# Fused attention and feed-forward: a fourth chunk in seven products, attention paced by weight, weight sums at the ends of two chunks

## The chip, the core and the metric

The kernel runs on one core of one Trainium2 chip. The metric is device time in microseconds (us) of one execution. TensorE (PE) multiplies matrices; VectorE (DVE), ScalarE (ACT) and GpSimd (POOL) do element-wise work; SyncE (SP) issues most DMA transfers, and ScalarE some. Each engine has a queue of its own; they wait for each other by semaphores.

## The reference, cut to what matters

```python
k_p = k.reshape(B, H, Sp, pool, D).mean(axis=3)      # 8 x 8 heads, 576 rows pooled to 72, D = 64
v_p = v.reshape(B, H, Sp, pool, D).mean(axis=3)
scores = scale * np.matmul(q, k_p.transpose(0, 1, 3, 2))
attn = softmax(scores)                               # with 1e-09 added to the sum
x = np.matmul(attn, v_p) -> 4608 tokens x 512        # heads side by side
h = x @ w_in                                         # 512 x 2048
g = np.maximum(0.01 * h, h)
return g @ w_out                                     # 2048 x 512
```

All data is fp32.

## The kernel before

**Feed-forward.** The 4608 tokens go in nine chunks of 512 (`CH`), c = 0 to 8. The hidden features are 16 blocks `f` of 128. A product with fp32 accuracy is three matmuls on two parts of each number (`h` and `l`: high and low): high by high, high by low, low by high. For one `f`, `m1` (L1143 to L1145) makes `ph` in 12 matmuls of 512 columns; ACT applies the leaky step (L1148) and casts to `gh` (L1151), DVE forms `gl` (L1152); two blocks later `m2` adds the block to the four output sums `acc` through `add_up` (L1354 to L1356), 12 matmuls of 512 columns.

**Seven products.** For the last chunks `m1` is replaced: two blocks `f` form a pair (8 `PAIRS`), and a 2 by 2 product of half-size blocks is made with seven products in place of eight (`product`, L1261: six matmuls of 256 columns each, 42 a pair). It needs sums of the weights, made once by `prepare`: sums on DVE (L1183) in the spare buffer `x_tail`, a cast on ACT (`high`, L1186), a subtraction on DVE (`low`, L1190), and stores to `kept` in DRAM (L1217), four results of two parts a pair. They are read back into `seat`s and weight buffers by `stream` (L1253, issued by ACT). The first run with seven products is `REST + FAST - 1`.

**Runs.** The program is a list of runs n = 0 to 11, with REST = 4: n = 5 is chunk 2, n = 8 chunk 5 ("the sixth"), n = 11 chunk 8. So with FAST = 6 the runs n = 9, 10 and 11 use seven products.

**Attention** is made one or two chunks ahead, in steps that a run issues between its matmuls: `lk`, `ku`, `lv`, `vu` load and pool k and v (POOL L265, L272; `vremsum` are the pooled rows left over, `v_parts` L522 and L524 split them), `q` and `qa` load and turn q, `s` makes scores `pss` (L600) and `e` (L610), `sb` normalizes to `at` on POOL and stores it as `rows` (L661), which come back turned as `blocks` (L670; `at` and `blocks` share three buffers). `pu` transposes `blocks` to `pp` (DVE L681, a buffer of the pool `five`, tag "o", which output tiles use too) and splits it into `pT_hi` (ACT L703) and `pT_lo` (DVE L706, L710). `au` multiplies `pT` with v to `pa` (PE L725 to L728), named by piece and head pair (`pa_0_2`), and ACT (L744) and DVE (L745) split it into the next chunk's `xh`, `xl`.

**What sets the order.** PE runs in the order of the program text, and from the first run with seven products on POOL and SP too. The order on ACT, DVE and, before that, SP and POOL is fixed at the build. An engine then takes its instructions strictly in its order. A run with three plain products has 64 beats (a beat is a part of a matmul group, about 1.5 us), one with seven 96. `PLAN` says for a run how many pairs' sums `prepare` makes in it and between which beats. Attention's steps are spread over the run by their count: step i of m comes when the beat reaches i/m of the run.

```python
PLAN = {REST + 1: (2, 10, 36), REST + 2: (3, 3, 34), REST + 3: (1, 3, 20), REST + 4: (2, 3, 34)}
```

In all four runs the sums lie in parts of x buffers that `free` finds unused, and all of a pair's stores are issued behind its last `low`.

Of the kernel before, what the change touches and what calls it, by code (L numbers as in the profile page):

```python
# [10 lines left out]
F32 = mybir.dt.float32  # L11
F32R = mybir.dt.float32r
# [12 lines left out]
def tile_pooled_attention_ffn(  # L25
# [9 lines left out]
    nc = tc.nc  # L35

    P = 128
# [32 lines left out]
    VIA = 2  # L70
    SPLIT = 8
    HALF = CH // 2
    FAST = 6
    NEAR = (FAST + 1) % 2


# [1095 lines left out]
    def prepare(j, places):  # L1172

        f0, f1 = PAIRS[j]
        (a11, a12), (a21, a22) = (
            [[ws[0, f].bitcast(F32)[:, part, half] for part in range(2)]
             for half in (slice(0, HALF), slice(HALF, DM))] for f in (f0, f1)
        )
        u, w = (x_tail[:, 2 * i : 2 * i + 2, :].rearrange("p k x -> p (k x)") for i in range(2))
        ADD, SUB = ALU.add, ALU.subtract  # L1180

        def do(out, a, b, op):
            nc.vector.tensor_tensor(out, a, b, op=op)  # L1183

        def high(i, of):
            nc.scalar.copy(places[i][0], of)  # L1186

        def low(i, of):
            h, l = places[i]
            nc.vector.tensor_tensor(l, of, h.bitcast(F32), op=SUB)  # L1190

        do(u, a21[0], a21[1], ADD)
        do(w, u, a22[0], ADD)
        yield
        do(w, w, a22[1], ADD)
        high(1, w)
        do(u, a11[0], u, SUB)
        yield
        do(u, u, a11[1], ADD)
        high(0, u)  # L1200
        low(1, w)
        yield
        do(w, w, a11[0], SUB)
        low(0, u)
        yield
        do(w, w, a11[1], SUB)
        high(2, w)
        do(u, a12[0], w, SUB)
        yield
        do(u, u, a12[1], ADD)  # L1210
        high(3, u)
        low(2, w)
        yield
        low(3, u)
        for i, parts_of in enumerate(places):
            for k, part in enumerate(parts_of):
                nc.sync.dma_start(kept[j, :, i, k, :], part.bitcast(F32))  # L1217
        if j < OPEN:
            with tc.issue_after(sent[-1].ins):
                nc.sync.dma_start(kept[j, :, 4], ws[0, f1].bitcast(F32)[:, :, HALF:])  # L1220
        yield

    def free(n, i):

        if n < REST + FAST - 2:
            return [(h[:, HALF:], l[:, HALF:]) for h, l in zip(*x_parts(runs[n][0] + 1))]
        side, part = (runs[n][0] + 2) % 2, "hl"[i % 2]
        x = [one.tile([P, CH], F32R, tag=f"x{part}{side}_{kk}", name=f"place{i}_{kk}") for kk in range(NK)]
        return [(y[:, :HALF], y[:, HALF:]) for y in x]
# [230 lines left out]
    for b in range(2, B):  # L1460
        for j, piece in enumerate(PIECES[b]):
            c = 2 + (2 * TAIL + S * (b - 2) + piece[0][0]) // CH
            beside[REST + c - 2].append((b, j))
    units = []

    def line_of(n, pieces):
        start = REST + FAST - 1
# [38 lines left out]
    for b, n in loads_at.items():  # L1506
        early[max(n, REST) - 1].append(b)

    PLAN = {REST + 1: (2, 10, 36), REST + 2: (3, 3, 34), REST + 3: (1, 3, 20), REST + 4: (2, 3, 34)}
    STEPS_OF = 7  # L1510
    left = list(range(len(PAIRS)))

    def sums_in(n):
        for i in range(PLAN[n][0]):
            yield from prepare(left.pop(0), free(n, i))

    at = 0
    for n, (c, fs, ts) in enumerate(runs[: REST + FAST - 1]):
        us = list(units[n])
        final = n == REST + FAST - 2  # L1520
        steps_in = None
        if n >= REST:
            nxt = n - REST + 2
            if nxt in waiting:
                us.insert(0, lambda nxt=nxt: carry(nxt))
            mid = len(us) // 2
            for b in early[n]:
                us[mid:mid] = [att[b]["lk"], att[b]["lv"]]
            if n == REST:

                us.insert(3 * len(us) // 4, fetch)
        beats, done, beat = (2 + len(ts) // 2) * len(fs), 0, 0
        forming, formed = (sums_in(n), 0) if n in PLAN else (None, 0)
        many, begin, until = PLAN.get(n, (0, 0, 1))
        behind = 10 if final else 4
        for f in fs:
            if n == 0:
                convert_to(14 + 2.8 * f)
            elif n == 1:
                convert_to(36)  # L1540
            elif n == 2:
                convert_to(36 + 2.5 * f)
            elif n == 3:
                convert_to(36 + 2.5 * SPLIT + 2 * (f - SPLIT))
                if f == 11:
                    for b in early[n]:
                        att[b]["lk"]()
                        att[b]["lv"]()
            if final and f == NF - 2:
                while done < len(us):  # L1550
                    us[done]()
                    done += 1
                steps_in = combine(c + 1)
                steps_in[0]()
                steps_in[1]()
            slots = [m1(at)] + ([m2(at - 2)] if at >= 2 else [])
            if n and f == fs[0]:

                slots.reverse()
            for slot in slots:  # L1560
                for _ in slot:
                    beat += 1
                    while done < min(len(us), len(us) * beat // (beats - behind)):
                        us[done]()
                        done += 1
                    while forming and formed < min(1, (beat - begin) / (until - begin)) * STEPS_OF * many:
                        formed += 1
                        with tc.issue_after(casts[-1].ins), tc.issue_after(lows[-1].ins):
                            next(forming, None)
            at += 1  # L1570
        while done < len(us):
            us[done]()
            done += 1
# [19 lines left out]
    for n in range(REST + FAST - 1, len(runs)):  # L1593
        c = runs[n][0]
        us = list(units[n])
        nxt = c + 1 if n + 1 < len(runs) else None
        hooks = None
        if nxt:
            if nxt in waiting:
                us.insert(0, lambda nxt=nxt: carry(nxt))  # L1600
        beat = done = 0
        for i, j in enumerate(going):
            final = i == len(going) - 1
            if final and nxt:
                while done < len(us):
                    us[done]()
                    done += 1
                hooks = combine(nxt)
                us, units[n + 1] = units[n + 1][:LEAD], units[n + 1][LEAD:]
                done, beat = 0, -2  # L1610
            then = None if final else going[i + 1]
            for _ in pair(n, c, j, then, old, hooks if final else None):
                beat += 1
                whole = 9 if final and nxt else BEATS - 15
                while done < min(len(us), len(us) * beat // whole):
                    us[done]()
                    done += 1
        going.reverse()
# [34 lines left out]
```

## Time and profile before

| what | us |
|---|---|
| three runs, median (lowest to highest) | 919.36 (918.85 to 920.59) |
| the profiled execution | 919.74 |
| its span, first to last instruction | 917.9 |
| PE busy | 886.1 |
| DVE, ACT, POOL busy | 516.0, 446.5, 221.4 |
| run n = 9 (seven products, with attention) | 96.30, granted clock 1.00 |

Busy time is the time in which an engine runs an instruction; what is left of the span, engine by engine, is waiting. The mean granted TensorE clock of the profiled execution is 0.993 of full speed. An instruction's row shows its start, its length, and, in brackets, how long the engine stood idle before it and what ended that.

### The profile page before, as it was taken

The page shows a single profiled execution, that of the slowest core. Times are in us where ns is not written, and L with a number is a line of the kernel's source. Part 1 is how long each engine was busy: PE and PEld are TensorE (multiplying, and loading weights), DVE is VectorE, ACT ScalarE, POOL GpSimd, SP SyncE. Part 2 cuts the span into 40 slices and gives each one's busy share as a digit, 9 for nine tenths or more (in the row PEclk, how much of TensorE's full clock was granted, in tenths as well). Part 3 has the DMA queues.
Part 4 walks back from the last instruction along what each step waited for, and adds up shares of the span by engine and source line. Part 5 has one row for each costly group of instructions (what it writes and reads, how often), then busy time and mean ns, then how long its engine had stood idle before and what let it go on. Part 6 is the DMA issues. An engine that isn't in the chain of part 4 may idle for free.

```text
span 917.9 us, 14149 instructions
## 1 busy us (share of the span) xinstructions
PE 886.1 (97%) x4731; PEld 763.0 (83%) x4731; DVE 516.0 (56%) x1229; ACT 446.5 (49%) x1397; POOL 221.4 (24%) x394
## 2 busy tenths in 40 slices
PE   5599999999999999999999999999999999999998
PEld 4478889788887888888888888888899899999997
DVE  6999569546376655764455437554664652442222
ACT  5788569435244534443444435453654554453322
POOL 4511110342525231512132132413320230010000
PEclk9889999999999999999999999999999999999999
DMA  9965231328357442734244417630784254425332
GB/s 263 314 198 177 61 78 47 83 62 201 97 164 174 113 90 75 210 97 112 54 135 113 107 27 202 169 89 1 205 210 129 72 161 123 139 78 161 104 113 71
DMA packets 157464, 116.53 MB, mean 127 GB/s; under 512 B 100688, under 2 KB 136016, under 8 KB 157392
## 3 DMA queue, kind: packets, MB, share of 16 engines
q1 hardware_dynamic: 145488, 90.86, 36.7%
q10 hardware_dynamic: 11904, 24.78, 9.0%
q8 instruction: 37, 0.61, 0.3%
q14 instruction: 35, 0.29, 0.1%
HBM read 85.07 MB, written 30.54 MB: 126 GB/s over the span
## 4 chain that ended last, share of the span: by engine, by line
PE 82%; DVE 7%; DMA 4%; ACT 3%; POOL 1%; issue 1%; SPq 1%; ACTq 0%; POOLq 0%; DVEq 0%
PE acc L1354 13%; PE acc L1356 12%; PE acc L1355 12%; PE ph L1143 8%; PE ph L1145 8%; PE ph L1144 8%; PE ends_y L1261 7%; PE ends_x L1261 5%; PE pss L600 3%; PE pa L726 1%; DMA kremraw<-in_k_dram 1%; ACT e L610 1%; PE pa L728 1%; PE pa L727 1%; DMA blocks<-rows 1%
## 5 line engine op out<-in xcount | busy, mean ns | idle before, releaser
L1354 PE MATMUL acc<-w,gh 128*128 128x512 f32 x576 | 228.3, 396 | 0.6 <-DVE o L1394 0.6
L1355 PE MATMUL acc<-w,gh 128*128 128x512 f32 x576 | 225.4, 391 | 0.0
L1356 PE MATMUL acc<-w,gl 128*128 128x512 f32 x576 | 224.9, 390 | 0.3 <-DVE gl L1292 0.3
L1143 PE MATMUL ph<-xh,w 128*128 128x512 f32 (+1 forms) x416 | 159.3, 383 | 0.3 <-DVE gl L1152 0.3
L1145 PE MATMUL ph<-xh,w 128*128 128x512 f32 (+1 forms) x416 | 156.1, 375 | 0.0
L1144 PE MATMUL ph<-xl,w 128*128 128x512 f32 (+1 forms) x416 | 156.0, 375 | 0.0
L1356 PEld LDWEIGHTS acc<-w,gl 128*128 128x128 f32 x576 | 108.2, 188 | 24.5 <-DVE gl L1292 0.8
L1354 PEld LDWEIGHTS acc<-w,gh 128*128 128x128 f32 x576 | 108.5, 188 | 19.8 <-issue 1.0
L1355 PEld LDWEIGHTS acc<-w,gh 128*128 128x128 f32 x576 | 108.5, 188 | 18.1
L610 ACT ACTIVATE e<-pss,red 128x72 f32<-128x72 f32 (+1 forms) x320 | 97.6, 329 | 37.8 <-DVE red L608 37.7
L1148 ACT ACTIVATE ph<-ph 128x512 f32<-128x512 f32 (+1 forms) x104 | 57.7, 555 | 93.7 <-PE ph L1145 92.9
L1152 DVE TENSOR_TENSOR gl<-ph,gh 128x512 fp32r<-128x512 f32 (+1 forms) x104 | 66.7, 642 | 57.8 <-ACT gh L1151 57.1
L644 POOL TENSOR_TENSOR at<-e,red 128x128 f32<-128x128 f32 (+1 forms) x120 | 50.6, 441 | 181.2 <-DVE red L641 83.7
L1145 PEld LDWEIGHTS ph<-xh,w 128*128 128x128 f32 x416 | 78.7, 189 | 14.2
L1143 PEld LDWEIGHTS ph<-xh,w 128*128 128x128 f32 x416 | 78.9, 190 | 14.0 <-DVE gl L1152 0.7
L1144 PEld LDWEIGHTS ph<-xl,w 128*128 128x128 f32 x416 | 78.9, 190 | 13.0
L610 ACT ACTIVATION_READ_ACCUMULATOR e<-pss,red 128x1 f32 (+1 forms) x320 | 68.8, 215 | 0.0
L681 DVE STREAM_TRANSPOSE pp<-blocks 128x384 f32<-128x384 f32 (+1 forms) x60 | 44.4, 759 | 42.5 <-DMA blocks<-rows 42.1
L703 ACT CAST pT_hi<-pp 128x384 fp32r<-128x384 f32 (+1 forms) x80 | 36.8, 479 | 57.8 <-DVE pp L681 54.2
L608 DVE TENSOR_REDUCE red<-pss 128x4 f32<-128x288 f32 (+1 forms) x80 | 35.8, 453 | 50.7 <-PE pss L600 49.5
L1151 ACT CAST gh<-ph 128x512 fp32r<-128x512 f32 (+1 forms) x104 | 57.8, 555 | 2.6
L600 PE MATMUL pss<-kT,qT 128*128 128x144 f32 x320 | 48.9, 294 | 4.0 <-DVE xl L745 2.1
(290 smaller groups left out, 1481.9 us busy)
## 6 DMA issues: line engine op xcount, KB each, us to landing
seat<-kept ACTq DMA_DIRECT2D x31, 512.0 KB
rows<-at SPq DMA_DIRECT2D x48, 192.0 KB
blocks<-rows SPq DMA_DIRECT2D x48, 192.0 KB
out_dram<-o SPq DMA_DIRECT2D x34, 256.0 KB
w_bits<-in_moe_w_in_dram SPq DMA_DIRECT2D x16, 512.0 KB
w_bits<-in_moe_w_out_dram SPq DMA_DIRECT2D x16, 512.0 KB
q<-in_q_dram SPq DMA_DIRECT2D x96, 64.0 KB
w<-kept ACTq DMA_DIRECT2D x21, 256.0 KB
```

The costliest lines, as they stand in the source:

```text
L600: nc.tensor.matmul(sc[:, 2 * SP * i : 2 * SP * (i + 1)], qT[:, p, :], kT[:, p, :, :].rearrange("d i s -> d (i s)"), start=True, stop=True,)
L610: ins = nc.scalar.activation(e[:n, h, :], scv[:n, h, :], AF.Exp, bias=mx[:n, h : h + 1], accum_out=sm[:n, h : h + 1],)
L1143: nc.tensor.matmul(ph, w[:, 0, ks], xh[kk][:, r], start=kk == 0, stop=False)
L1144: nc.tensor.matmul(ph, w[:, 0, ks], xl[kk][:, r], start=False, stop=False)
L1145: nc.tensor.matmul(ph, w[:, 1, ks], xh[kk][:, r], start=False, stop=kk == NK - 1)
L1148: nc.scalar.activation(ph, ph, AF.Prelu, alpha=0.01)
L1151: casts.append(nc.scalar.copy(gh, ph))
L1152: lows.append(nc.vector.tensor_tensor(gl, ph, gh.bitcast(F32), op=ALU.subtract))
L1261: nc.tensor.matmul(out, w[:, stay, ks], move, start=start and i + n == 0, stop=i + n == 3, skip_group_check=True,)
L1354: nc.tensor.matmul(a, gh[:, r], hi, start=first, stop=False)
L1355: nc.tensor.matmul(a, gh[:, r], lo, start=False, stop=False)
L1356: nc.tensor.matmul(a, gl[:, r], hi, start=False, stop=last)
```

## The change

FAST becomes 5, so run n = 8 (chunk 5) becomes the first with seven products. `prepare` may be called without places; then it takes a tile of the pool `five`, tag "o", for each result. Each result's two parts are stored as soon as `low` has run. `PLAN` gives n = 5 two pairs at beats 51 to 63 with such tiles, n = 6 two at 6 to 36 in free parts of x buffers and two at 47 to 63 with tiles, n = 7 two at 3 to 34; n = 8 has none. In the runs with seven products a step of attention is released by weight (34 for `s`, 21 for `pu`, and so on) and not by count.

```diff
@@ -70,7 +70,7 @@
     VIA = 2
     SPLIT = 8
     HALF = CH // 2
-    FAST = 6
+    FAST = 5
     NEAR = (FAST + 1) % 2
 
 
@@ -1183,11 +1183,16 @@
             nc.vector.tensor_tensor(out, a, b, op=op)
 
         def high(i, of):
+            if places[i] is None:
+                o = five.tile([P, 2, HALF], F32R, tag="o", name=f"place{j}_{i}")
+                places[i] = o[:, 0], o[:, 1]
             nc.scalar.copy(places[i][0], of)
 
         def low(i, of):
             h, l = places[i]
             nc.vector.tensor_tensor(l, of, h.bitcast(F32), op=SUB)
+            for k, part in enumerate(places[i]):
+                nc.sync.dma_start(kept[j, :, i, k, :], part.bitcast(F32))
 
         do(u, a21[0], a21[1], ADD)
         do(w, u, a22[0], ADD)
@@ -1212,9 +1217,6 @@
         low(2, w)
         yield
         low(3, u)
-        for i, parts_of in enumerate(places):
-            for k, part in enumerate(parts_of):
-                nc.sync.dma_start(kept[j, :, i, k, :], part.bitcast(F32))
         if j < OPEN:
             with tc.issue_after(sent[-1].ins):
                 nc.sync.dma_start(kept[j, :, 4], ws[0, f1].bitcast(F32)[:, :, HALF:])
@@ -1462,6 +1464,10 @@
             c = 2 + (2 * TAIL + S * (b - 2) + piece[0][0]) // CH
             beside[REST + c - 2].append((b, j))
     units = []
+    WEIGHT = {"s": 34, "sb": 7, "qa": 11, "ku": 12, "vu": 14, "pu": 21, "au": 12}
+    weight = {
+        id(u): WEIGHT.get(name.rstrip("0123456789"), 2) for one_of in att for name, u in one_of.items()
+    }
 
     def line_of(n, pieces):
         start = REST + FAST - 1
@@ -1506,13 +1512,13 @@
     for b, n in loads_at.items():
         early[max(n, REST) - 1].append(b)
 
-    PLAN = {REST + 1: (2, 10, 36), REST + 2: (3, 3, 34), REST + 3: (1, 3, 20), REST + 4: (2, 3, 34)}
+    PLAN = {REST + 1: [(2, 51, 63, False)], REST + 2: [(2, 6, 36, True), (2, 47, 63, False)], REST + 3: [(2, 3, 34, True)]}
     STEPS_OF = 7
     left = list(range(len(PAIRS)))
 
-    def sums_in(n):
-        for i in range(PLAN[n][0]):
-            yield from prepare(left.pop(0), free(n, i))
+    def sums_in(n, which):
+        for i in range(which[0]):
+            yield from prepare(left.pop(0), free(n, i) if which[3] else [None] * 4)
 
     at = 0
     for n, (c, fs, ts) in enumerate(runs[: REST + FAST - 1]):
@@ -1530,8 +1536,7 @@
 
                 us.insert(3 * len(us) // 4, fetch)
         beats, done, beat = (2 + len(ts) // 2) * len(fs), 0, 0
-        forming, formed = (sums_in(n), 0) if n in PLAN else (None, 0)
-        many, begin, until = PLAN.get(n, (0, 0, 1))
+        forming = [[which, sums_in(n, which), 0] for which in PLAN.get(n, ())]
         behind = 10 if final else 4
         for f in fs:
             if n == 0:
@@ -1563,10 +1568,12 @@
                     while done < min(len(us), len(us) * beat // (beats - behind)):
                         us[done]()
                         done += 1
-                    while forming and formed < min(1, (beat - begin) / (until - begin)) * STEPS_OF * many:
-                        formed += 1
-                        with tc.issue_after(casts[-1].ins), tc.issue_after(lows[-1].ins):
-                            next(forming, None)
+                    for turns in forming:
+                        many, begin, until, _ = turns[0]
+                        while turns[2] < min(1, (beat - begin) / (until - begin)) * STEPS_OF * many:
+                            turns[2] += 1
+                            with tc.issue_after(casts[-1].ins), tc.issue_after(lows[-1].ins):
+                                next(turns[1], None)
             at += 1
         while done < len(us):
             us[done]()
@@ -1599,6 +1606,9 @@
             if nxt in waiting:
                 us.insert(0, lambda nxt=nxt: carry(nxt))
         beat = done = 0
+        reached = [0]
+        for u in us:
+            reached.append(reached[-1] + weight.get(id(u), 5))
         for i, j in enumerate(going):
             final = i == len(going) - 1
             if final and nxt:
@@ -1608,11 +1618,12 @@
                 hooks = combine(nxt)
                 us, units[n + 1] = units[n + 1][:LEAD], units[n + 1][LEAD:]
                 done, beat = 0, -2
+                reached = range(len(us) + 1)
             then = None if final else going[i + 1]
             for _ in pair(n, c, j, then, old, hooks if final else None):
                 beat += 1
                 whole = 9 if final and nxt else BEATS - 15
-                while done < min(len(us), len(us) * beat // whole):
+                while done < len(us) and reached[done] * whole < reached[len(us)] * beat:
                     us[done]()
                     done += 1
         going.reverse()
```

The change is seen in the order of instructions at three places. Numbers behind names tell buffers apart, `place` is a tile for sums, and what a row waits for stands in brackets.

The first place is on VectorE, near the end of n = 5, between gl of block 13 and the first use of pT for pa_0_2. Before:

```order
L1152 TENSOR_TENSOR gl_13_3628<-ph_13_3613,gh_13_3627 128x512 [waits PE_49,Activation_49]
L745 TENSOR_TENSOR xl_1_2962<-pa_0_1_3638,xh_1_2958 128x320 [waits DMAHW0_49,Activation_49]
L706 TENSOR_TENSOR pT_lo<-pp_0_1_3653,pT_hi 128x2x128 [waits PE_49,Activation_49]
L710 SCALAR_TENSOR_TENSOR pT_hi<-pp_0_1_3653,marks,pT_hi 128x128 [waits PE_49]
L706 TENSOR_TENSOR pT_lo<-pp_1_1_3673,pT_hi 128x2x128 [waits Activation_49]
L710 SCALAR_TENSOR_TENSOR pT_hi<-pp_1_1_3673,marks,pT_hi 128x128
L706 TENSOR_TENSOR pT_lo<-pp_2_1_3691,pT_hi 128x2x64 [waits Activation_49]
L710 SCALAR_TENSOR_TENSOR pT_hi<-pp_2_1_3691,marks,pT_hi 128x64
```

After:

```order
L1152 TENSOR_TENSOR gl_13_3588<-ph_13_3567,gh_13_3587 128x512 [waits PE_49,Activation_49]
L1183 TENSOR_TENSOR x_tail<-x_tail,w_4_657 128x256 [waits DVE_49]
L1193 TENSOR_TENSOR place_0_3575<-x_tail,place_0_3575 128x256
L745 TENSOR_TENSOR xl_1_3178<-pa_0_1_3598,xh_1_3174 128x320 [waits Activation_49]
L706 TENSOR_TENSOR pT_lo<-pp_0_1_3617,pT_hi 128x2x128 [waits PE_49,Activation_49]
L710 SCALAR_TENSOR_TENSOR pT_hi<-pp_0_1_3617,marks,pT_hi 128x128 [waits PE_49]
L1183 TENSOR_TENSOR x_tail<-x_tail,w_4_657 128x256 [waits DVE_49]
L1183 TENSOR_TENSOR x_tail<-w_4_657,x_tail 128x256 [waits DVE_49]
L1193 TENSOR_TENSOR place_2_3623<-x_tail,place_2_3623 128x256 [waits DMAHW6_49,DMAHW5_49,Activation_49]
L1183 TENSOR_TENSOR x_tail<-x_tail,w_4_657 128x256 [waits DVE_49]
L681 STREAM_TRANSPOSE pp_1_1_3647<-blocks_1_1_3645 128x4x96 [waits DMAHW7_49,DMAHW3_49,DMAHW0_49]
L1193 TENSOR_TENSOR place_3_3633<-x_tail,place_3_3633 128x256 [waits Activation_49]
```

Four sums (L1183), three `low`s (L1193, L1190 before) and the transposes pp_1_1 and, just behind these rows, pp_2_1 (which waits for three DMAs too) now stand between gl_13 and the last pT steps; pp_1_1 now waits for two more DMAs.

The second place is the end of n = 6, ahead of pa_0_0, on ScalarE. Before:

```order
L703 CAST pT_hi<-pp_0_0_4538 128x3x128 [waits DVE_49]
L703 CAST pT_hi<-pp_1_0_4551 128x3x128 [waits DVE_49]
L1148 ACTIVATE ph_11_4480<-ph_11_4480 128x512 [waits PE_49]
L1151 CAST gh_11_4494<-ph_11_4480 128x512 [waits Activation_49]
L1148 ACTIVATE ph_12_4518<-ph_12_4518 128x512 [waits PE_49]
L1151 CAST gh_12_4532<-ph_12_4518 128x512 [waits Activation_49]
L522 ACTIVATE v_parts<-vremsum_4260 128x128 [waits Pool_49]
L1148 ACTIVATE ph_13_4562<-ph_13_4562 128x512 [waits DVE_49,PE_49]
```

After:

```order
L1189 CAST place_1_4511<-x_tail 128x256 [waits DMAHW6_49,DVE_49]
L703 CAST pT_hi<-pp_0_0_4527 128x3x128 [waits DVE_49]
L1148 ACTIVATE ph_12_4503<-ph_12_4503 128x512 [waits PE_49]
L1151 CAST gh_12_4521<-ph_12_4503 128x512 [waits Activation_49]
L1189 CAST place_0_4533<-x_tail 128x256 [waits DVE_49]
L522 ACTIVATE v_parts<-vremsum_4246 128x128 [waits Pool_49]
L703 CAST pT_hi<-pp_1_0_4546 128x3x128 [waits DVE_49]
L1189 CAST place_2_4562<-x_tail 128x256 [waits DMAHW5_49,DMAHW2_49,DVE_49]
L1148 ACTIVATE ph_13_4565<-ph_13_4565 128x512 [waits PE_49]
L744 CAST xh_0_3865<-pa_0_0_4589 128x256 [waits DMAHW1_49,PE_49]
```

The cast pT_hi of pp_1_0 moved from five rows ahead of `v_parts` to behind it. On VectorE, the same stretch. Before:

```order
L706 TENSOR_TENSOR pT_lo<-pp_1_0_4551,pT_hi 128x2x128 [waits Activation_49]
L710 SCALAR_TENSOR_TENSOR pT_hi<-pp_1_0_4551,marks,pT_hi 128x128
L1152 TENSOR_TENSOR gl_11_4495<-ph_11_4480,gh_11_4494 128x512 [waits PE_49,Activation_49]
L1152 TENSOR_TENSOR gl_12_4533<-ph_12_4518,gh_12_4532 128x512 [waits PE_49,Activation_49]
L524 SCALAR_TENSOR_TENSOR vremsum_4260<-vremsum_4260,v_parts 128x128 [waits Activation_49]
L527 TENSOR_SCALAR vremsum_4260<-vremsum_4260,signs 128x128 [waits DVE_49]
```

After:

```order
L1193 TENSOR_TENSOR place_1_4511<-x_tail,place_1_4511 128x256
L681 STREAM_TRANSPOSE pp_1_0_4546<-blocks_1_0_4544 128x4x96 [waits DMAHW6_49,DVE_49]
L1183 TENSOR_TENSOR x_tail<-x_tail,w_8_1108 128x256 [waits DVE_49]
L1193 TENSOR_TENSOR place_0_4533<-x_tail,place_0_4533 128x256 [waits Activation_49]
L524 SCALAR_TENSOR_TENSOR vremsum_4246<-vremsum_4246,v_parts 128x128 [waits Activation_49]
L1183 TENSOR_TENSOR x_tail<-x_tail,w_8_1108 128x256 [waits DVE_49]
L706 TENSOR_TENSOR pT_lo<-pp_1_0_4546,pT_hi 128x2x128 [waits Activation_49]
L710 SCALAR_TENSOR_TENSOR pT_hi<-pp_1_0_4546,marks,pT_hi 128x128
```

pT_lo of pp_1_0, which stood ahead of the gl of block 11, now stands behind L524, which waits for `v_parts`.

The third place is on SP, in the same stretch, around the loads of `vremraw`. Before:

```order
L670 DMA blocks_1_0_4549<-rows_1_0_4425 128x384 [waits DMAHW6_49,DMAHW2_49]
L670 DMA blocks_0_1_4606<-rows_0_1_4307 128x384 [waits DMAHW7_49,DMAHW3_49,DVE_49]
L670 DMA blocks_1_1_4620<-rows_1_1_4510 128x384 [waits DMAHW5_49,DMAHW0_49]
L318 DMA vremraw_4273<-in_v_dram 32x1x512 [waits DMAHW1_49,Pool_49]
L318 DMA vremraw_4273<-in_v_dram 32x1x512 x2
```

After:

```order
L661 DMA rows_1_1_4493<-at_1_1_4489 128x4x96 [waits DMAHW5_49,Pool_49]
L670 DMA blocks_1_0_4544<-rows_1_0_4408 128x384 [waits DMAHW6_49,DMAHW2_49]
L670 DMA blocks_0_1_4618<-rows_0_1_4295 128x384 [waits DMAHW7_49,DMAHW5_49]
L318 DMA vremraw_4259<-in_v_dram 32x1x512 [waits DMAHW0_49,Pool_49]
L318 DMA vremraw_4259<-in_v_dram 32x1x512 [waits DMAHW1_49]
...
L1195 DMA kept<-place_1_4511 128x256 [waits DMAHW2_49,Activation_49]
L670 DMA blocks_1_1_4634<-rows_1_1_4493 128x384 [waits DMAHW3_49,DVE_49]
```

blocks_1_1 moved behind the loads and behind a store of a sum, and blocks_0_1 waits for DMA queue 5, on which the row of rows_1_1 stands first here.

## Rows read from the trace of the kernel before

**Rows 1.** The page: busy us, share of the span and instructions of each engine.

```profile
PE 886.1 (97%) x4731; PEld 763.0 (83%) x4731; DVE 516.0 (56%) x1229; ACT 446.5 (49%) x1397; POOL 221.4 (24%) x394
```

**Rows 2.** PE's waits by releaser: us in total, times, longest us.

```profile
PE pa L726 <- DVE pT_lo L706: 2.8, 3, 1.6
...
PE pa L725 <- ACT pT_hi L703: 0.9, 2, 0.5
...
PE acc L1354 <- DVE o L1394: 0.6, 1, 0.6
...
PE ph L1143 <- DVE gl L1152: 0.3, 1, 0.3
```

**Rows 3.** Windows, n = 9: start:end, us; PE, PEld, DVE, ACT, POOL busy; clock; DMA; GB/s.

```profile
638.90:735.20 96.30, 95.48 (x610) 86.32 (x609) 56.61 (x138) 51.39 (x181) 18.14 (x38) 1.00 0.54 147
```

**Rows 4.** Timeline of PE in n = 8 and n = 10, stretches without attention.

```profile
627.79 0.39 PE L1143 MATMUL ph<-xh,w 128*128 128x512 f32 x1
...
638.67 0.39 PE L1588 MATMUL ends_y<-w 128*128 128x512 f32 x1
...
777.86 0.28 PE L1261 MATMUL ends_y<-B227xh,seat 128*128 128x256 f32 x1
...
777.98 0.28 PE L1261 MATMUL ends_y<-B227xl,seat 128*128 128x256 f32 x1
...
788.40 0.28 PE L1261 MATMUL ends_y<-B227xh,seat 128*128 128x256 f32 x1
```

**Rows 5.** Timeline of PE, then DVE, early in n = 5.

```profile
290.66 0.28 PE L725 MATMUL pa<-pT_hi,v_hi 128*128 128x256 f32 x1
...
292.59 0.38 PE L726 MATMUL pa<-pT_lo,v_hi 128*128 128x256 f32 x1 [1.65 <-DVE pT_lo L706]
...
288.99 1.41 DVE L1183 TENSOR_TENSOR x_tail<-w,x_tail 128x256 f32<-128x256 f32 x1
...
290.86 0.62 DVE L706 TENSOR_TENSOR pT_lo<-pp,pT_hi 128x256 fp32r<-128x256 f32 x1
```

**Rows 6.** Timeline of PE, then DVE, near the end of n = 5.

```profile
342.66 0.31 PE L725 MATMUL pa<-pT_hi,v_hi 128*128 128x320 f32 x1
...
336.08 0.68 DVE L1152 TENSOR_TENSOR gl<-ph,gh 128x512 fp32r<-128x512 f32 x1
...
338.46 0.28 DVE L710 SCALAR_TENSOR_TENSOR pT_hi<-pp,marks,pT_hi 128x64 fp32r<-128x64 f32 x1
```

**Rows 7.** Groups by line on DVE, n = 5: count, busy us, mean ns, idle before.

```profile
L1183 DVE TENSOR_TENSOR x_tail<-x_tail,w 128x256 f32<-128x256 f32 x12 | 5.6, 463 | 0.1
...
L1190 DVE TENSOR_TENSOR xl<-x_tail,xh 128x256 fp32r<-128x256 f32 x8 | 4.0, 498 | 0.0
```

**Rows 8.** The chain that ended last, in order of time, start of n = 6.

```profile
363.40 3.29 DMA out_dram<-o
```

**Rows 9.** Timeline of SP, POOL, ACT, DVE and PE, end of n = 6.

```profile
413.86 0.57 SPq L661 DMA_DIRECT2D rows<-at  x1
...
416.45 0.32 SPq L670 DMA_DIRECT2D blocks<-rows  x1
...
418.70 0.32 SPq L670 DMA_DIRECT2D blocks<-rows  x1
...
419.11 5.40 SPq L318 DMA_DIRECT2D vremraw<-in_v_dram  x8
...
429.71 2.11 POOL L265 TENSOR_TENSOR vremraw<-vremraw 128x512 f32<-128x512 f32 x2 [11.70 <-DMA k0raw<-in_k_dram]
...
433.03 0.46 POOL L272 TENSOR_TENSOR vremsum<-vremraw 128x128 f32<-128x128 f32 x1
...
433.52 0.31 ACT L522 ACTIVATE v_parts<-vremsum 128x128 fp32r<-128x128 f32 x1 [7.93 <-POOL vremsum L272]
...
433.86 0.47 DVE L524 SCALAR_TENSOR_TENSOR vremsum<-vremsum,v_parts 128x128 f32<-128x128 f32 x1 [7.55 <-ACT v_parts L522]
...
429.75 0.28 PE L726 MATMUL pa<-pT_lo,v_hi 128*128 128x256 f32 x1
```

## The prediction

> **What bounds the kernel now.** I read the page's busy times first [rows 1]: TensorE works 886.1 of 917.9 us. The list of TensorE's waits comes next [rows 2]; after the start-up its items are small, the largest 2.8 us in three waits. So the time is TensorE's own instructions plus a few stalls, and a change pays only if it shortens TensorE's program or moves a stall. VectorE and ScalarE have room on average, even where attention and seven products share a chunk (56.61 and 51.39 of 96.30 us [rows 3]); but each takes its instructions in the order that the build fixed, and one late operand holds up everything behind it. The rest is therefore a search for places where a different order makes TensorE wait. The profiled execution is 919.74 us, of which 917.9 are span; the median of the runs is 919.36, so I add to 919.74 and take off 0.38 at the end.
>
> **The change part by part.**
>
> *Seven products in one more chunk.* [Rows 4] have both kinds without attention between. Two hidden blocks of 128 features the plain way go from 627.79 to 638.67: 48 matmuls of 512 columns in 10.88 us, 0.2267 us each. One pair with seven products goes from 777.86 to 788.40: 42 matmuls of 256 columns and 24 of 512 in 10.54 us. The pair saves 0.34 us, and the chunk has eight: **−2.8**. This is far less than the missing columns suggest (eight products' worth become seven in the first half, an eighth of 5.44 us, 0.68 a pair), because a 256-column matmul takes more than half of a 512-column one. The Trainium skill ("TensorE: Matmul & The Clock Gate", section "Back-to-back issue gap") gives an isolated gap of N/2.4 + 2.5 ns, 109 ns for 256 columns and 216 for 512. By it the chunk would save 4.7 us, estimated from that page alone. The trace differs: consecutive 256-column matmuls of one pair start about 0.12 us apart, and 48 of 512 take 10.88 us and not 10.4; the measurement decides.
>
> *The weight sums leave the start of run n = 5.* There TensorE stood 1.65 us at 292.59 for pT_lo, and VectorE shows why [rows 5]: behind the transposes came a sum of 1.41 us (288.99) and a subtraction of `prepare`, and only then, at 290.86, the pT_lo that TensorE wanted right after its matmul of 290.66. With the sums gone from there pT_lo comes over 1.5 us sooner: **−1.65**.
>
> *They now stand at the end of n = 5* (the first order piece). TensorE asks for the second group's pT at 342.66; VectorE had finished it at 338.74 [rows 6], so 3.9 us of room. Four sums and three `low`s of 0.46 and 0.50 us [rows 7] now stand ahead, 3.4 us: they just fit. But pp_1_1 and pp_2_1 take buffers in which weight sums lie that must first be stored. From gl_13 (336.08, ends 336.76) to the end of `low(2)` there are eight instructions of about 0.46 us, so 340.4; the nearest landing that I have is 3.29 us, a store of out_dram [rows 8], behind an issue of 0.3 to 0.6 (SP's in [rows 9]). That gives 344.3, and with pp_2_1 and four small pT steps (about 1.6) 345.9: a stall of up to 3.2 us. With stores that land at once it is nothing. I take the middle, **+1.7** (0 to 3.2), as one row of a store to another place cannot say more.
>
> *Start of n = 6.* acc waited 0.6 us for an output tile at 367.7 [rows 2], whose buffer was held by the store at 363.40 [rows 8]. The sums beside it start three beats later and one store fewer stands ahead on SP: **−0.5** (0 to −0.6).
>
> *End of n = 6*, the largest unknown (the order pieces of ScalarE, VectorE and SP). On ScalarE the step L522 `v_parts` waited until 433.52 for POOL's vremsum, 7.93 us; on VectorE L524 waited 7.55 behind it [rows 9]. Both stalls cost nothing, because pT for pa_0_0 had been made ahead of them and TensorE ran pa_0_0 at 429.6. After the change the cast pT_hi of pp_1_0 stands *behind* v_parts on ScalarE, and its pT_lo behind L524 and a sum on VectorE. TensorE is in program order and needs all 256 columns of that group: pa_0_0 must now wait for vremsum. If vremsum is as late as before, pT_lo ends at 433.86 + 0.47 + 0.46 + 0.46 = 435.25, against 429.75 in the trace: 5.5 us. What could bring it forward are the eight loads of vremraw, since blocks_1_1 moves behind them on SP. That transfer was issued at 418.70 and the one ahead of it at 416.45: at best the loads start 2.25 us sooner, and 3.2 us remain. But the new order has blocks_0_1 wait for the store of rows_1_1 (it takes over that tile's buffer), which is what I read as having held 418.70, so much of the gain may be missing. Behind pa_0_0 queue the acc matmuls of the same run, nothing else can go first. I take **+4.2** (3.2 to 5.5).
>
> *Run n = 8 as a mixed run.* It now has batch 7's loads, five or six tiles of attention and seven products, as n = 9 had. That one lost 96.30 − 95.48 = 0.8 us in small waits [rows 3], among them two for pT_hi of up to 0.5 [rows 2]. Old n = 8 had one of 0.3 (ph for gl [rows 2]); n = 7 now has its load of sums and may keep it. Steps by weight leave the distance from the pT steps to the pa matmuls much as it was by the order of TensorE. **+0.25** (−0.3 to +0.8). The extra reads of kept weights (a chunk with seven products keeps the DMA engines 0.54 busy at most [rows 3]) I cost at nothing; they lie beside TensorE's 10.5 us pairs.
>
> **Sum:** −2.8 − 1.65 + 1.7 − 0.5 + 4.2 + 0.25 = +1.2; 919.74 + 1.2 − 0.38 = **920.6 us**. The 0.2% that a measurement of this kernel can tell from no change is 1.8 us.
>
> **The rivals.**
>
> 1. *No loss at the end of n = 6: faster.* If vremsum came before TensorE asks, the sum falls by 4.2 to −3.0, 916.4, and with no buffer wait at the end of n = 5 either to 914.7. For it: the loads take ten of these microseconds from the first issue (419.11) to POOL's start (429.71), far more than their issues, so a little less traffic ahead of them might count for more than its issue. Against: POOL had waited 11.70 us for them [rows 9]; they would have to be 5.5 us earlier, where one transfer fewer ahead is worth 2.25. Between lies the case that both terms are at their low ends (3.2 and 0): 917.9, on the border.
> 2. *The v_parts wait at full price: slower.* The loads keep their old start, 5.5 instead of 4.2, and the sums' landings cost 3.2 at the end of n = 5: each alone gives about 922, both 923.4. From +4.8 us at v_parts on, with the rest as summed, the kernel is slower by more than 0.2%. For it: blocks_0_1's wait as above. Against: each of these needs the upper end of its range.
> 3. *256-column matmuls at their isolated gap.* The page's rule would take 1.9 us more off than the row, 918.7. The trace has 1008 such matmuls at about 0.12 us; I give it 0.02.
>
> **How the numbers follow.** Likeliest is that the saved products and the gone stall are paid back by the two new waits: 0.39, with 918.8 to 921.2 its own range. Rival 1 has 0.27, rival 2 has 0.32, rival 3 0.02. So faster by over 0.2% 0.27, within 0.41, slower 0.32. The range 916.0 to 923.0 leaves out the part of rival 1 in which both waits are nearly gone, and the last few tenths of rival 2.
>
> **What would show it.** Right: TensorE's program ends with 10.54 us pairs from the sixth chunk on and that chunk is about 2.8 us shorter than its matmuls were; no wait of pa L726 near 290; a wait of pa L725 or L726 for pT at about 341 to 345, and one at 429 to 434 of 3 us or more, with ScalarE idle before v_parts until then. Wrong: vremsum done before 429, or POOL's wait for the loads much shorter than 11.7 us; a pair of the new mixed run that takes over 10.7 us beyond its attention matmuls; or new waits in n = 7 and n = 8 for gl, seats or qT that add up to more than 1 us, for which no row here gives a price.

## The result

The changed kernel takes **931.0 us** (median of 6 runs, 928.85 to 935.85) against 920.3 (6 runs) for the kernel before: a ratio of 1.0122, 95% interval 1.0103 to 1.0141. It is slower by 1.2%, above the range of the prediction. Its profiled execution, the fastest of the six, has a span of 927.0 us, 9.1 more than before; what is read from the trace below accounts for these 9.1 us.

The page of the changed kernel: busy us by engine, then the chain that ended last by engine.

```profile
PE 889.0 (96%) x4875; PEld 771.0 (83%) x4875; DVE 530.1 (57%) x1244; ACT 458.7 (49%) x1428; POOL 229.4 (25%) x398
...
PE 77%; DVE 6%; DMA 6%; SPq 3%; ACT 3%; POOL 2%; issue 2%; ACTq 0%; POOLq 0%; DVEq 0%
```

TensorE's busy time rose by 2.9 us [rows 1] although its matmuls now have fewer columns in all, and its share of the chain fell from 82% to 77%: DMA (4% before) and SP's queue (1%) took most of that. TensorE's waits, first those that are new or larger than before [rows 2]:

```profile
PE pa L725 <- ACT pT_hi L703: 7.8, 4, 3.9
...
PE pa L726 <- DVE pT_lo L706: 2.4, 4, 0.9
...
PE ph L1143 <- DVE gl L1152: 1.4, 3, 0.8
...
PE ends_y L1263 <- DVE ends_y L1313: 0.7, 1, 0.7
```

pT_hi was waited for 0.9 us before and 7.8 now. Where this lies the windows show, one for each of the runs n = 5 to n = 9 (us; PE, PEld, DVE, ACT, POOL busy; granted clock; DMA share; GB/s):

```profile
262.00:356.00 94.00, 92.75 (x439) 77.77 (x438) 53.51 (x134) 39.03 (x129) 28.09 (x49) 1.00 0.47 121
356.00:451.00 95.00, 91.84 (x420) 75.80 (x420) 61.48 (x152) 40.95 (x130) 25.06 (x44) 0.98 0.48 134
451.00:547.00 96.00, 95.49 (x453) 80.17 (x452) 56.85 (x140) 46.55 (x152) 31.10 (x53) 1.00 0.41 110
547.00:650.00 103.00, 98.06 (x609) 88.61 (x608) 59.20 (x138) 51.48 (x182) 35.45 (x58) 0.97 0.63 166
650.00:742.00 92.00, 91.31 (x586) 82.97 (x585) 54.29 (x132) 48.40 (x165) 17.96 (x37) 1.00 0.55 155
```

In the windows of n = 6 and n = 8 TensorE stands idle for 3.2 and 4.9 us, and in both its granted clock is under 1.00 (0.98 and 0.97); n = 9 of the kernel before, the run most like the new n = 8, had 1.00 [rows 3].

**n = 5.** The stall at the early pa is gone (a row of 290.13 without a bracket, against [rows 5]), and one has come near its end, as forecast:

```profile
290.13 0.28 PE L726 MATMUL pa<-pT_lo,v_hi 128*128 128x256 f32 x1
...
341.49 0.42 PE L725 MATMUL pa<-pT_hi,v_hi 128*128 128x320 f32 x1 [1.25 <-ACT pT_hi L703]
```

**End of n = 6.** Timeline of SP, POOL, ACT, DVE and PE:

```profile
416.92 3.41 SPq L318 DMA_DIRECT2D vremraw<-in_v_dram  x5
...
426.31 2.20 POOL L265 TENSOR_TENSOR vremraw<-vremraw 128x512 f32<-128x512 f32 x2 [9.63 <-DMA vremraw<-in_v_dram]
...
430.05 0.63 POOL L272 TENSOR_TENSOR vremsum<-vremraw 128x128 f32<-128x128 f32 x1
...
430.71 0.31 ACT L522 ACTIVATE v_parts<-vremsum 128x128 fp32r<-128x128 f32 x1 [3.80 <-POOL vremsum L272]
...
430.93 0.49 ACT L703 CAST pT_hi<-pp 128x384 fp32r<-128x384 f32 x1
...
431.77 0.41 DVE L706 TENSOR_TENSOR pT_lo<-pp,pT_hi 128x256 fp32r<-128x256 f32 x1
...
431.47 0.38 PE L725 MATMUL pa<-pT_hi,v_hi 128*128 128x256 f32 x1 [1.85 <-ACT pT_hi L703]
...
432.24 0.39 PE L726 MATMUL pa<-pT_lo,v_hi 128*128 128x256 f32 x1 [0.38 <-DVE pT_lo L706]
```

vremsum comes at 430.68, v_parts at once, pT_hi of pp_1_0 behind it, then pT_lo: TensorE waits 1.85 and 0.38 us and loses 2.65 us against an even pitch (0.12 us from one of these matmuls to the next). The loads started 2.2 us earlier than before [rows 9]. What the prediction did not count follows:

```profile
431.00:433.00 2.00, 1.15 (x6) 0.95 (x7) 1.95 (x7) 0.42 (x2) 0.36 (x1) 0.94 0.30 59
433.00:435.00 2.00, 2.00 (x8) 1.71 (x8) 0.24 (x1) 0.12 (x1) 0.00 (x0) 0.50 1.07 302
435.00:437.00 2.00, 2.00 (x8) 1.57 (x7) 1.66 (x4) 2.00 (x6) 0.03 (x1) 0.71 0.64 222
```

The granted clock falls to 0.50, the 1.2 GHz level, right behind the stall: 0.94, 0.50 and 0.71 in three stretches of 2 us, which costs another 2 x (0.06 + 0.50 + 0.29) = 1.7 us while TensorE is busy all the time from 433 on.

**n = 8.** Its first matmul and that of n = 9, then two starts of the same product, a pair apart, with eight score matmuls of attention between:

```profile
546.85 0.28 PE L1263 MATMUL ends_x<-B115xh,w 128*128 128x256 f32 x1
...
650.11 0.28 PE L1263 MATMUL ends_x<-B116xh,w 128*128 128x256 f32 x1
...
637.14 0.28 PE L1263 MATMUL ends_y<-B225xh,seat 128*128 128x256 f32 x1
...
648.68 0.28 PE L1263 MATMUL ends_y<-B225xh,seat 128*128 128x256 f32 x1
```

The run takes 103.3 us. The pair itself is as fast as forecast (11.54 us with the eight score matmuls; a pair without attention took 10.54 in the kernel before, [rows 4]). The time goes at one place, around 606 us:

```profile
607.34 0.37 DVE L681 STREAM_TRANSPOSE pp<-blocks 128x192 f32<-128x192 f32 x1
...
605.66 0.39 ACTq L1255 DMA_DIRECT2D w<-kept  x1
...
606.08 0.62 ACT L1293 CAST gh<-dia 128x512 fp32r<-128x512 f32 x1 [2.43 <-DMA rows<-at]
...
608.81 0.33 ACTq L1255 DMA_DIRECT2D seat<-kept  x1
...
609.17 0.62 ACT L1293 CAST gh<-off 128x512 fp32r<-128x512 f32 x1 [1.98 <-DMA v0raw<-in_v_dram]
...
609.70 0.35 ACT L703 CAST pT_hi<-pp 128x192 fp32r<-128x192 f32 x1
...
610.10 0.53 PE L725 MATMUL pa<-pT_hi,v_hi 128*128 128x320 f32 x1 [3.86 <-ACT pT_hi L703]
...
611.52 0.63 PE L726 MATMUL pa<-pT_lo,v_hi 128*128 128x320 f32 x1 [0.89 <-DVE pT_lo L706]
```

Here ScalarE is the one to look at. It issues the loads of kept weights itself (ACTq). Up to 605.66 and 608.81 it stood before such an issue; gh waited 2.43 and 1.98 us behind it, and pT_hi of the last tile, whose pp was there at 607.71, came only at 609.70. TensorE waited 3.86 us for pT_hi and 0.89 for pT_lo. The brackets name what the issues waited for: two transfers that SP had issued, rows and v0raw, had to land. The chain that ended last, followed back within 600 to 612, has the second:

```profile
601.46 7.33 DMA v0raw<-in_v_dram
```

The windows there:

```profile
602.00:606.00 4.00, 4.00 (x28) 3.63 (x26) 1.09 (x3) 0.42 (x1) 0.97 (x3) 1.00 1.02 246
606.00:610.00 4.00, 0.24 (x3) 0.03 (x1) 1.16 (x3) 1.94 (x4) 1.08 (x1) 1.00 1.09 236
610.00:618.00 8.00, 7.01 (x27) 6.31 (x28) 2.29 (x5) 2.50 (x8) 1.24 (x2) 0.57 0.45 99
```

The DMA engines are full (1.02 and 1.09) with the 256 KB loads of v for batch 7, with rows, blocks and kept weights, and when TensorE goes on the clock is 0.57 for 8 us: up to 3.4 us more (8 x 0.43; TensorE was busy for 7.0 of the 8).

### The profile page after: what moved, and what is told of

Read it like the earlier page. It is cut to its first block, busy times and chain, and to the rows that moved or that the text cites. A ratio compares the mean times of both kernels' runs of the same rounds, so it can differ in the third digit from the quotient of the medians.

```text
span 927.0 us, 14514 instructions
## 1 busy us (share of the span) xinstructions
PE 889.0 (96%) x4875; PEld 771.0 (83%) x4875; DVE 530.1 (57%) x1244; ACT 458.7 (49%) x1428; POOL 229.4 (25%) x398
## 4 chain that ended last, share of the span: by engine, by line
PE 77%; DVE 6%; DMA 6%; SPq 3%; ACT 3%; POOL 2%; issue 2%; ACTq 0%; POOLq 0%; DVEq 0%
PE acc L1356 12%; PE acc L1357 12%; PE acc L1358 12%; PE ends_y L1263 9%; PE ends_x L1263 7%; PE ph L1143 6%; PE ph L1145 6%; PE ph L1144 6%; PE pss L600 3%; DMA blocks<-rows 2%; DMA vremraw<-in_v_dram 1%; PE pa L726 1%; SPq L318 1%; PE pa L728 1%; PE pa L727 1%
## 5 line engine op out<-in xcount | busy, mean ns | idle before, releaser
L1143 PE MATMUL ph<-xh,w 128*128 128x512 f32 (+1 forms) x352 | 134.2, 381 | 1.4 <-DVE gl L1152 1.4
L1144 PE MATMUL ph<-xl,w 128*128 128x512 f32 (+1 forms) x352 | 131.1, 372 | 0.0
L1145 PE MATMUL ph<-xh,w 128*128 128x512 f32 (+1 forms) x352 | 131.0, 372 | 0.0
L1148 ACT ACTIVATE ph<-ph 128x512 f32<-128x512 f32 (+1 forms) x88 | 48.5, 551 | 69.2 <-PE ph L1145 68.8
L1152 DVE TENSOR_TENSOR gl<-ph,gh 128x512 fp32r<-128x512 f32 (+1 forms) x88 | 56.0, 636 | 41.6 <-ACT gh L1151 37.8
L1143 PEld LDWEIGHTS ph<-xh,w 128*128 128x128 f32 x352 | 66.8, 190 | 13.5 <-DVE gl L1152 2.7
L1145 PEld LDWEIGHTS ph<-xh,w 128*128 128x128 f32 x352 | 66.7, 189 | 11.7
L1144 PEld LDWEIGHTS ph<-xl,w 128*128 128x128 f32 x352 | 66.8, 190 | 10.5
L1294 DVE TENSOR_TENSOR gl<-off,gh 128x512 fp32r<-128x512 f32 x32 | 22.3, 697 | 52.6 <-ACT gh L1293 52.6
L600 PEld LDWEIGHTS pss<-kT,qT 128*128 128x128 f32 x320 | 45.8, 195 | 7.6 <-issue 1.7
```

Source lines behind the costliest of these rows:

```text
L600: nc.tensor.matmul(sc[:, 2 * SP * i : 2 * SP * (i + 1)], qT[:, p, :], kT[:, p, :, :].rearrange("d i s -> d (i s)"), start=True, stop=True,)
L1143: nc.tensor.matmul(ph, w[:, 0, ks], xh[kk][:, r], start=kk == 0, stop=False)
L1144: nc.tensor.matmul(ph, w[:, 0, ks], xl[kk][:, r], start=False, stop=False)
L1145: nc.tensor.matmul(ph, w[:, 1, ks], xh[kk][:, r], start=False, stop=kk == NK - 1)
L1148: nc.scalar.activation(ph, ph, AF.Prelu, alpha=0.01)
L1152: lows.append(nc.vector.tensor_tensor(gl, ph, gh.bitcast(F32), op=ALU.subtract))
```

## The experiments

All are the changed kernel with one or a few edits; times are medians, ratios are to the kernel before (919.6 us) on the same chip, 95% interval in brackets. Beside the changed kernel the kernel before took 920.3 us, so a difference from 931.0 is uncertain by some 0.7 us. An entry of the new `PLAN` is (pairs, first beat, last beat, True for parts of x buffers or False for tiles).

**1. No late sums in n = 6.**

```diff
-PLAN = {..., REST + 2: [(2, 6, 36, True), (2, 47, 63, False)], REST + 3: [(2, 3, 34, True)]}
+PLAN = {..., REST + 2: [(2, 6, 36, True)], REST + 3: [(2, 3, 34, True), (2, 36, 62, False)]}
```

> The changed kernel, but the two pairs of sums at the end of n = 6 stand at beats 36 to 62 of n = 7. The cast pT_hi of pp_1_0 is then ahead of v_parts again. Theory: TensorE's 2.65 us of stall at pa_0_0 of n = 6 and the 3.4 us at the half granted clock behind it (worth 1.7) go: about 926.5 us against 931.0. Rival (vremsum or pT would be late there anyway, and the clock falls for another reason): 930 to 931.

927.35 us, 1.0086 (1.0064 to 1.0108). The sums in n = 7 overwrite tokens that are carried in x_tail, so part of the output differs; the instructions are as many. The timeline of PE has the same pa with no wait, and the windows the full clock:

```profile
430.51 0.28 PE L725 MATMUL pa<-pT_hi,v_hi 128*128 128x256 f32 x1
...
430.63 0.28 PE L726 MATMUL pa<-pT_lo,v_hi 128*128 128x256 f32 x1
...
433.00:435.00 2.00, 2.00 (x11) 1.65 (x10) 2.00 (x7) 1.03 (x3) 0.00 (x0) 1.00 0.81 227
```

So the stall and the slow clock of n = 6 come from the sums that stand beside v_parts. The median falls by 3.7 of the 4.4 us (its interval still touches that of the changed kernel, so it is the trace that shows this): pa in n = 7 now waits 0.66 and 0.49 us for pT_hi.

**2. v's loads later in the mixed run.** `KV` gives the slots of the steps that load and pool the next batch; the last four are those of v.

```diff
-KV = {0: 1, 1: 2, 2: 3, 3: 4, 4: 5, 5: 6, 6: 8}
+KV = {0: 1, 1: 2, 2: 3, 3: 8, 4: 9, 5: 10, 6: 12}
```

> The changed kernel, but in the runs with seven products the four steps that load and pool v of the next batch come four to five slots later. Theory: in n = 8 these 256 KB loads fill the DMA engines at 602 to 612 us, so that blocks come late and the seat loads on ScalarE's queue hold up its pT_hi; without them there the stall of 5.3 us at pa and the slow clock behind it (3.4) go, at least by half: 922 to 927 us. Rival (the stream of kept weights beside rows and blocks is too much by itself, or the wait moves on to another step): 930 to 933.

925.16 us, 1.0063 (1.0042 to 1.0085): 5.8 us less than the changed kernel, as expected. The windows at the same place:

```profile
602.00:606.00 4.00, 4.00 (x27) 3.63 (x26) 1.95 (x6) 1.70 (x4) 1.15 (x3) 1.00 0.84 280
606.00:610.00 4.00, 4.00 (x27) 3.67 (x26) 1.37 (x3) 3.21 (x9) 0.00 (x0) 1.00 0.41 116
610.00:618.00 8.00, 8.00 (x54) 7.33 (x53) 5.33 (x12) 2.56 (x6) 0.00 (x0) 1.00 0.64 167
```

TensorE has no idle time there and the full clock; the DMA share is 0.84 and 0.41. The wait did move, but shrank: 0.90 us for pT_hi at 619, and 1.16 for kT in n = 9.

**3. Attention by count.**

```diff
-            reached.append(reached[-1] + weight.get(id(u), 5))
+            reached.append(reached[-1] + 1)
```

> The changed kernel, but attention's steps in the runs with seven products are released by count, as before the change. Theory: the weights move steps by fractions of a pair, so 929 to 933 us and the stall in n = 8 stays within 2 us. Rival (the weights put pT too near to its use): 922 to 926 and no stall over 2 us in n = 8.

928.42 us, 1.0085 (1.0062 to 1.0109). My theory was wrong here: the stall at pa in n = 8 shrinks to 0.30 us although v's loads are issued where they were (54.4 us into the run, 53.9 in the changed kernel), and 2.15 us of wait for kT appear at 574.

```profile
610.23 0.41 PE L725 MATMUL pa<-pT_hi,v_hi 128*128 128x320 f32 x1 [0.30 <-ACT pT_hi L703]
```

So the weights take part in the stall. In this order the loads also came in sooner: from SP's last issue for v0raw to POOL's start on it, for which POOL stood waiting in both runs, it is 3.4 us here and 6.9 in the changed kernel, with a DMA share of 0.64 against 1.02 from 602 to 606.

**4. FAST = 6, sums as changed.**

```diff
-    FAST = 5
+    FAST = 6
```

> The changed kernel with FAST = 6: three chunks in seven products as before, but the new places of the weight sums. Theory: what the sums lost and gained stays (-1.8 early in n = 5, +1.4 at its end, -0.8 and +1.2 early in n = 6, +2.65 and 1.7 of slow clock at its end), so about 924.5 us against 920.3 before. Rival (the loss is all in n = 8 and the sums' places cost nothing): 919 to 921.

923.58 us, 1.0044 (1.003 to 1.0058). The new places of the sums (with the steps by weight in the last three runs, which stay) cost 4.0 us; the rest of the loss, 7.4 us net of the products, is in n = 8 and behind it. The late pT_hi of n = 6 is there again:

```profile
431.26 0.38 PE L725 MATMUL pa<-pT_hi,v_hi 128*128 128x256 f32 x1 [2.02 <-ACT pT_hi L703]
```

**5. Who holds pT_hi in n = 8?** The loads of kept weights go to SP:

```diff
-                    stream(nc.scalar, then, name)
+                    stream(nc.sync, then, name)
```

> The changed kernel, but the kept weights are loaded by SP and no longer by ScalarE. Theory: part of the stall in n = 8 is ScalarE standing at its own DMA issues (605.66 and 608.81), with gh and pT_hi behind them; then pT_hi follows pp at once, the stall of 5.3 us at pa falls to about 2, and the time to 924 to 929. Rival (the blocks come late in any case, and SP now has the kept weights' waits ahead of them): 930 or more, with pp later than before.

927.9 us, 1.008 (1.0061 to 1.0099), with a stall at the end of n = 6 that was 4.87 us in the profiled execution, longer than elsewhere. In n = 8 the same tile now goes through (DVE, ACT, PE):

```profile
611.50 0.38 DVE L681 STREAM_TRANSPOSE pp<-blocks 128x192 f32<-128x192 f32 x1
...
611.90 0.35 ACT L703 CAST pT_hi<-pp 128x192 fp32r<-128x192 f32 x1 [1.05 <-DVE pp L681]
...
612.57 0.31 PE L725 MATMUL pa<-pT_hi,v_hi 128*128 128x320 f32 x1
...
550.39 0.28 PE L1263 MATMUL ends_x<-B115xh,w 128*128 128x256 f32 x1
...
648.78 0.28 PE L1263 MATMUL ends_x<-B116xh,w 128*128 128x256 f32 x1
```

pT_hi follows pp by 0.4 us (2.4 us in the changed kernel), and pa starts with no wait. The run n = 8 takes 650.11 − 546.85 = 103.3 us in the changed kernel and 648.78 − 550.39 = 98.4 here, although it now has waits of 2.21 and 0.24 us for the weights themselves.

This run moved more than the issues. SP, which now stands before the loads of weights too, issued v0raw only 59.3 us into the run (53.9 in the changed kernel), and the DMA share from 602 to 610 was 0.76 and 0.67. That ScalarE's own issues held pT_hi is shown by the rows of the changed kernel: pp was there at 607.71, and ScalarE did nothing until its issue at 608.81. That the transfers it waited for landed late because the DMA engines were full is argued from the windows: experiments 2 and 5 both moved v's loads and the traffic together.

**6. Can the change be made to pay?** Sums in the middle of n = 5 and one pair in tiles of its own in n = 7 (first diff), with v's loads late as in experiment 2, then with the loads where the change has them, then with late loads and by count as in experiment 3; last, FAST = 6 with the sums of the kernel before, but the first two pairs later (second diff); steps by weight stay.

```diff
+PLAN = {REST + 1: [(2, 22, 46, True)], REST + 2: [(3, 3, 34, True)], REST + 3: [(2, 3, 34, True), (1, 34, 44, False)]}
```

```diff
+PLAN = {REST + 1: [(2, 22, 46, True)], REST + 2: [(3, 3, 34, True)], REST + 3: [(1, 3, 20, True)], REST + 4: [(2, 3, 34, True)]}
```

> The changed kernel with the sums placed anew (n = 5: two pairs at beats 22 to 46 in x buffers; n = 6: three at 3 to 34 in x buffers; n = 7: two at 3 to 34 in x buffers and one at 34 to 44 in tiles of its own) and v's loads late as in the run of v's loads. Theory: both losses go, the product's gain of 2.8 and the 1.65 early in n = 5 stay, small waits in n = 8 and n = 9 take some 3 us more than before: 916 to 919, against 919.6 before. Rival (a chunk with batch 7's loads and seven products is slower than the plain chunk wherever sums and loads stand): 921 or more.

> As the run before, but v's loads where the change has them. Theory: the stall at pa in n = 8 and the slow clock behind it are back: 5 to 7 us more than with late loads, 921 to 925. Rival (the late loads won by chance of the sums' places): within 2 us of it.

> As the first of these, but attention's steps by count. Theory: within 3 us of it, since weights move steps by fractions of a pair, but which small waits remain in n = 8 and n = 9 changes. Rival (the weights are a gain of their own): over 3 us slower than it.

> The kernel before in seven products for three chunks, its sums where they were but for n = 5: two pairs at beats 22 to 46 in place of 10 to 36 (and each store right behind its subtraction). Theory: only the stall of 1.65 us at pa early in n = 5 goes: 917.5 to 919, faster by 0.1 to 0.25%. Rival (the sums in the later beats make a stall of their own): 919.6 or more.

923.8 us (1.0032 to 1.007), 929.0 (1.009 to 1.0155), 920.9 (1.0005 to 1.0027) and 918.2 (0.9979 to 1.0002). The late loads are worth 5.2 us again, though in the profiled executions 1.7 of the difference is a slow clock in n = 7, ahead of those loads (last section).

The first expectation was missed by 5 us, with a time on its rival's side (921 or more): the pair of sums in n = 7 made pa wait for pT_hi there, 2.02 us ahead of 522.97, as the two pairs had done at the end of n = 6. The rival's reason, that the chunk is slower wherever sums and loads stand, falls with experiment 7. Steps by count gave 2.9 us more, so with late loads the weights are no gain; without them (experiment 3) the medians went the same way by 2.6 us, with overlapping intervals.

The last one shows that the early stall of n = 5 can be removed without the rest, for 1.3 us that its interval does not tell from nothing: pa waited 0.68 us at the next group, and 1.58 us of wait for gl came up in n = 8.

**7. All sums in x buffers, v's loads late, by count; and the sixth chunk alone undone.** Three pairs in n = 5 (first line) or four in n = 6 (second line); and the first of these with FAST = 6.

```diff
+PLAN = {REST + 1: [(3, 20, 46, True)], REST + 2: [(3, 3, 34, True)], REST + 3: [(2, 3, 34, True)]}
+PLAN = {REST + 1: [(2, 22, 46, True)], REST + 2: [(4, 3, 36, True)], REST + 3: [(2, 3, 34, True)]}
```

> The changed kernel with all sums in x buffers and none late (n = 5: three pairs at beats 20 to 46; n = 6: three at 3 to 34; n = 7: two at 3 to 34), v's loads late and attention by count. Theory: the third pair no longer disturbs n = 7 (3.9 us of waits in the run with one pair in tiles of its own there), so 916.5 to 918.5 against 919.6 before. Rival (three pairs in n = 5 make waits of their own as long): 919.6 or more.

> As the run before, but two pairs in n = 5 (beats 22 to 46) and four in n = 6 (3 to 36). Theory: 916.5 to 919; the sums cost nothing so long as they end before beat 36 of n = 6. Rival (four pairs keep VectorE so busy that gl or output tiles come late): 920 or more.

> The first of these with FAST = 6, so three chunks in seven products: the sixth chunk alone is undone. Theory: that chunk's products are worth 2.8 us once nothing waits, less what its mixed run loses in small waits (1 to 2 us): 0.8 to 2.8 us slower than the first of these. Rival (seven products in that chunk are worth nothing even then): the same within 0.5 us, or faster.

919.46 us, 0.9987 (0.9972 to 1.0001); **916.38 us, 0.9958 (0.9942 to 0.9974)**; and 921.43 us, 1.0014 (1.0002 to 1.0025). Undoing only the sixth chunk costs 2.0 us, as the theory had it (2.8 less small waits). The first time is 1 us above its expectation: with three pairs in n = 5 pa of that run waits 1.29 and 1.14 us, and the clock falls behind it (0.50 from 333 to 335). With four in n = 6 only 0.91 of it is left, and the clock stays. Of that kernel, the first matmul of n = 8 and of n = 9, and the waits for pT:

```profile
541.16 0.28 PE L1263 MATMUL ends_x<-B115xh,w 128*128 128x256 f32 x1
...
636.37 0.28 PE L1263 MATMUL ends_x<-B116xh,w 128*128 128x256 f32 x1
...
PE pa L726 <- DVE pT_lo L706: 2.0, 3, 0.9
...
PE pa L725 <- ACT pT_hi L703: 0.3, 1, 0.3
```

n = 8 takes 636.37 − 541.16 = 95.2 us, 8 us less than in the changed kernel. This version beats both kernels. It keeps the fourth chunk of seven products, but neither the weights nor the late sums.

## Why the prediction was wrong

**What held.** The products: the pair in the trace has the forecast pitch, and the chunk was worth 2.0 us when undone by itself. The early stall of n = 5 went (−1.65). The one at its end is 1.25 us, forecast +1.7. acc's wait for an output tile went (−0.6), but two waits for gl of 0.17 and 0.75 us came in its place. The end of n = 6 happened as described, but with 2.65 us against 4.2 forecast, below the term's own range of 3.2 to 5.5. The loads started 2.2 us sooner, nearly the most that I had allowed, and vremsum came 2.8 us sooner (433.49 before, 430.68 now). I had read POOL's 11.70 us as a wait for the eight loads alone; the row in [rows 9] names k0raw, issued behind them, while in the changed kernel the same wait ends with vremraw. In the other runs with late sums in n = 6 the same stall was up to 5 us.

**The step that failed** is "Run n = 8 as a mixed run", set at +0.25 with a range to +0.8. It was priced from n = 9 of the kernel before, as a run with the same contents. It was not: batch 7's loads of v had been in n = 8 then, beside plain products, where ScalarE issues no DMA; POOL, which pools them, was busy for 18.14 us in the old n = 9 [rows 3] and for 35.45 in the new n = 8. (One of the two waits for pT_hi that I put into the old n = 9 was not there either, but at 52.46, near the start.) Put beside seven products, the loads of v share queues and DMA engines with kept weights that ScalarE itself loads, and the engine that makes pT stands still until SP's transfers have landed. I had named "the extra reads of kept weights" and cost them at nothing by the share of the whole run (0.54); in the 8 us that mattered it was above 1. The sentence that steps by weight leave the distance from pT to pa much as it was failed too: by count the same stall is 0.30 us (experiment 3).

In place of +0.25 the runs showed a stall of 4.75 us (3.86 and 0.89), and with the clock near 8 us: the run takes 103.3 us, 96.8 where only the loads moved (experiment 2) and 95.2 in the last version.

**What no term had** is the clock behind a stall: 1.7 us in n = 6 and up to 3.4 in n = 8. Each stall was priced as idle time alone.

From the parts: −2.8 − 1.65 + 1.25 − 0.6 + 0.9 + 2.65 + 1.7 for the sums and products, 4.75 + 3.4 in n = 8, and 0.7 of a new wait of the products (ends_y for L1313) are 10.3 us. The spans differ by 9.1: 3.4 is a ceiling, and small waits of the kernel before went (0.3 in n = 8, 0.8 in n = 9), while one of 0.5 for gl came in n = 7. The second rival (slower by v_parts) had the right side by luck: its price for that wait was 5.5 us, and the wait was shorter than even the likeliest case had it. None of the three rivals had the stall in n = 8.

What stays open: why v's loads land sooner with steps by count, and whether full DMA engines or the mere place of a load ahead of ScalarE's issue makes it wait. No run moved one without the other.

## What to carry to other kernels

When work moves into a stage of another kind, list what that stage has of its own on every queue, DMA issues of compute engines first, and price it for the microseconds where they meet, not by the mean share of the stage. A wait on a queue in program order is safe only as long as nothing that the bottleneck needs stands behind it: v_parts waited 7.93 us in the kernel before and cost nothing; in the changed kernel it waited 3.80, with one cast for TensorE behind it, and that cost 4.4 (2.65 of stall and 1.7 of slow clock). Price a stall of the matrix engine with the slow clock that may follow.

## What the hardware showed that I had not expected

The length of a wait did not decide by itself whether TensorE's granted clock fell behind it. Two runs of experiment 6 show it best, at the same place in n = 7. With late loads TensorE waited 2.02 and 0.70 us, and the clock stayed at 1.00; with the loads where the change has them it waited 2.04 and 0.71 us, and the clock was 0.84, 0.50 and 0.80 in the three stretches of 2 us from 523 on, worth 1.7 us. The stretch from 525 to 527 in the first and in the second:

```profile
525.00:527.00 2.00, 2.00 (x11) 1.67 (x10) 1.66 (x4) 1.58 (x5) 1.16 (x1) 1.00 0.00 0
525.00:527.00 2.00, 2.00 (x7) 1.69 (x7) 1.64 (x4) 1.69 (x5) 1.00 (x1) 0.50 0.00 0
```

It also fell to 0.50 after waits of 1.85 and 0.38 us in the changed kernel, and after one of 1.54 us in the run by count (near the end of n = 5):

```profile
343.00:345.00 2.00, 2.00 (x6) 1.53 (x5) 1.98 (x6) 0.64 (x3) 0.00 (x0) 0.50 0.12 43
```

After 1.25 us at the same place in the changed kernel, after 1.65 us in n = 5 of the kernel before [rows 5], and after 2.15 us at 574 in the run by count it stayed at 1.00. What decides was not found here.
